# Two layers of windowed attention and MLP on one core: all queues, homes and PSUM banks in a new order, with K's weights and products ahead of Q's

## The chip, the core and the metric

The kernel runs on one core of a Trainium2 chip. Its time is the device time of one execution in microseconds (us); the time of a kernel is the median of several executions.

## The reference

```python
# x: 1 x 2048 x 512 bf16; 32 heads of 16; window W = 256; F = 1792
def A(x, wqkv, wo):                       # sliding-window attention
    q, k, v = split(x @ wqkv)             # each 32 x 2048 x 16
    s = q @ k.T * 16 ** -0.5
    mask = (i - j >= 0) & (i - j < 256)   # query i, key j
    return softmax(where(mask, s, -1e9)) @ v  -> heads joined -> @ wo
def B(x, w1, b1, w2, b2):                 # dense MLP
    return gelu_tanh(x @ w1 + b1) @ w2 + b2
x = A_x
for _ in range(2):                        # the same weights twice
    x = x + A(layernorm(x), wqkv, wo)
    x = x + B(layernorm(x), w1, b1, w2, b2)
```

## The kernel before

The 2048 rows are 16 tiles of 128; two layers make 32 tiles, taken in 16 blocks of two tiles (256 queries). All weights and the activations X stay in SBUF in bf16; sums are made in PSUM, in 8 banks of 512 fp32 columns.

For each block, `lnq` makes the layernorm of X (VectorE's statistics, the reciprocal root on GpSimd, the normalised `xn` on VectorE), transposes it (by DMA; on TensorE for tiles 0 to 3 of the first layer and for the last two of the kernel) into `xnTA`, and multiplies it by Q's weights; `kv` does the same for K and V. One group of Q or of K is 8 products of 256 columns into one bank (L653, operands `Wqkv_sb` and `xnTA`), V is 4 products of 512 columns a tile. Q and V are copied out of PSUM by VectorE or ScalarE (L588, L590); K is copied and masked to even and odd heads by VectorE (L687). `Vs`, V with its halves of 64 rows exchanged, is made by DMA (L702).

`attention(b)` runs score visits: a visit takes four banks in two pairs, makes 512 columns of scores for each of four row groups (L754: products of 64 to 256 columns on 32 rows, four of them side by side), then one exponential on ScalarE for each pair (L761, 128 x 1024), which frees the pair, and a multiplication by 0/1 masks on VectorE or GpSimd (L782). After five visits (three in the first block of a layer) P x V runs for one half of the heads (L804, on rows 64 at a time), VectorE transposes the result out of PSUM (L813), takes reciprocals of the sums (L817), normalises (L821, VectorE or GpSimd) and transposes again; then the output product with `Wo_sb` is added to X (L849) and the second layernorm follows.

`mlp(J)` takes jobs of 2 or 4 tiles (`JOBS`): 14 hidden chunks (L653, `W1_sb` and `xnTB`), of which six go through VectorE's bias addition (L871) and three GELUs of two chunks each, and eight through ScalarE's GELU with bias straight from PSUM (L879). Each output tile is 14 products (L653, `W2_sb` and `gT`, 512 columns) added by VectorE to `Xb` (L894), X plus the second bias; in the second layer it is then written to the output. The last tile is split into two halves of 256 columns. ScalarE's exponentials and GELUs need different tables, so they are grouped: the order has 19 changes of table.

Before the first real product TensorE runs 18 warm-up products of zeros (L539, `warm`, 32 or 512 columns).

No loop sets the order in which all this reaches the engines. The code above only adds nodes to a plan (`_Plan.add`), 3098 of them, and three tables written out by hand set the rest. `_Plan.run` applies them:

```python
for i in _ALT:
    nodes[i]["eng"], nodes[i]["fn"] = nodes[i]["alts"][1]
banks = iter(_BANKS)
for i in _ORDER:
    ...
    for g, k in nd["alloc"]:
        b = next(banks)
        gmap[g] = tuple(range(b, b + k))
```

`_ORDER` is one global order of the nodes; each engine's queue is what that order holds for it. `_ALT` names the nodes that go to their second home: a copy of Q, V or a transposed tile from VectorE to ScalarE, a mask or a normalisation from VectorE to GpSimd, an addition of epsilon from GpSimd to VectorE. `_BANKS` gives each allocation in PSUM its bank, or the first of its pair. `_Sched.op` then adds the semaphore waits that reads, writes and reused banks need, in that order; so an engine waits in its queue where what it needs is late, and all behind it on that engine waits too.

## Time and profile before

| | before |
|---|---|
| median of 3 runs | 442.46 us (442.39 to 442.56) |
| span of the profiled execution | 442.4 us |
| TensorE (PE) busy | 416.1 us, 94% |
| ScalarE (ACT) busy | 386.4 us, 87% |
| VectorE (DVE) busy | 341.0 us, 77% |
| GpSimd (POOL) busy | 212.7 us, 48% |

The profile is of one execution, on this one core. PEld is TensorE's loading of weights, which overlaps its products; SP is the engine whose queue issues the DMAs. In a row of a group, `out<-in` names the tensors, then come partitions x elements and the type, the count, busy time in us and the mean of one in ns, and behind the second bar the idle time just before the group's instructions with what ended most of it. In a row of the timeline stand the start in us, the busy time, the engine, the line, the operation, and in brackets the wait and its releaser. Where a row says `W_sb`, it is W1, W2 or a part of them. The records hold nearly all products of TensorE.

### The profile page before, as it was taken

To read this page: it belongs to the slowest core of one execution; us is meant where nothing else is said; L and a number is where in the kernel's file an instruction comes from. 1 tells how busy PE (TensorE), PEld (TensorE's weight loads), DVE (VectorE), ACT (ScalarE), POOL (GpSimd) and SP (SyncE) were. 2 spreads that over 40 slices of the span, in tenths; PEclk is the share of its full clock that TensorE was granted. 3 is DMA by queue.
4 is the path that set the end of the run, shared out by engine and by line. 5 is a ranking of instruction groups with operands and counts; after the bars stand their busy time and mean duration, and the time that the engine had idled before them with its cause. 6 is when DMAs were issued, how large, how long until landed. Compare 5 with 4: busy or idle time off the path is not lost.

```text
span 442.4 us, 16864 instructions
## 1 busy us (share of the span) xinstructions
PE 416.1 (94%) x7523; PEld 233.2 (53%) x7593; DVE 341.0 (77%) x638; ACT 386.4 (87%) x458; POOL 212.7 (48%) x236
## 2 busy tenths in 40 slices
PE   8997999988789997999999999999999999999997
PEld 4555657544444563554455455455555464444675
DVE  7997789788785599967698868877888576746762
ACT  4997999999889999889899989999897988999533
POOL 3566344363442674711575454634728165804411
PEclk9999999999899999999999999999999999999999
DMA  7686422004101012121031021100421014003002
GB/s 234 184 209 185 87 64 45 20 10 69 39 3 25 16 34 56 28 46 24 4 65 31 1 57 26 34 20 10 69 39 20 20 39 105 14 1 81 15 0 73
DMA packets 48116, 23.25 MB, mean 53 GB/s; under 512 B 33196, under 2 KB 48044, under 8 KB 48044
## 3 DMA queue, kind: packets, MB, share of 16 engines
q1 hardware_dynamic: 48044, 22.17, 22.2%
q8 instruction: 60, 0.98, 0.9%
q14 instruction: 12, 0.10, 0.1%
HBM read 8.00 MB, written 2.10 MB: 23 GB/s over the span
## 4 chain that ended last, share of the span: by engine, by line
PE 79%; ACT 11%; DVE 6%; issue 2%; DMA 1%; DVEq 0%
PE ps L653 59%; PE ps L754 9%; PE ps L804 9%; ACT E L761 9%; DVE OD L813 1%; PE ps L539 1%; DVE stat L599 1%; DVE X L849 1%; DMA xnTB<-xn 1%; ACT gT L879 1%; ACT L879 1%; DVE KT L687 1%; DVE E L782 0%; PE ps L639 0%; ACT QT L590 0%
## 5 line engine op out<-in xcount | busy, mean ns | idle before, releaser
L761 ACT ACTIVATE E<-ps 128x1024 bf16<-128x1024 f32 x300 | 284.2, 1033 | 28.7 <-PE ps L754 28.0
L782 POOL TENSOR_TENSOR E<-E,mask 128x512 bf16<-128x512 bf16 (+2 forms) x111 | 120.9, 1106 | 91.3 <-ACT E L761 91.0
L653 PE MATMUL ps<-W_sb,gT 128*128 128x512 bf16 (+1 forms) x434 | 112.2, 373 | 3.2 <-issue 2.2
L653 PE MATMUL ps<-xnTB,W_sb 128*128 128x512 bf16 (+1 forms) x541 | 107.8, 336 | 3.4 <-issue 1.8
L653 PEld LDWEIGHTS ps<-xnTB,W_sb 128*128 128x128 bf16 x560 | 52.0, 98 | 42.9 <-issue 4.1
L653 PE MATMUL ps<-xnTA,Wqkv_sb 128*128 128x256 bf16 x512 | 70.7, 273 | 0.9 <-ACT E L761 0.4
L782 DVE TENSOR_TENSOR E<-E,mask 128x512 bf16<-128x512 bf16 (+2 forms) x125 | 60.1, 500 | 13.3 <-ACT E L761 12.9
L754 PE MATMUL ps<-QT,KT 32*128 32x128 bf16 (+3 forms) x1920 | 60.3, 231 | 9.8 <-ACT E L761 5.6
L653 PEld LDWEIGHTS ps<-W_sb,gT 128*128 128x128 bf16 x462 | 41.2, 98 | 41.1 <-issue 3.6
L754 PEld LDWEIGHTS ps<-QT,KT 32*128 32x128 bf16 x1920 | 28.5, 92 | 59.1 <-ACT E L761 34.9
L653 PEld LDWEIGHTS ps<-xnTA,Wqkv_sb 128*128 128x128 bf16 x512 | 47.4, 98 | 20.2 <-issue 2.9
L813 DVE STREAM_TRANSPOSE OD<-ps 128x1024 f32<-128x1024 f32 x32 | 39.9, 1246 | 21.3 <-PE ps L804 20.7
L887 POOL TENSOR_TENSOR Xb<-X,b2all 128x512 f32<-128x512 bf16 x32 | 37.7, 1180 | 34.3 <-DVE X L894 33.9
L879 ACT ACTIVATE gT<-ps,b1T 128x512 bf16<-128x512 f32 (+1 forms) x80 | 42.6, 609 | 9.5 <-PE ps L653 9.4
L804 PE MATMUL ps<-E,Va 64*17 64x128 bf16 (+3 forms) x1920 | 44.3, 234 | 1.9 <-issue 0.8
L821 POOL TENSOR_TENSOR Nb<-OD,Rc 128x512 bf16<-128x512 f32 x25 | 26.4, 1058 | 38.7 <-DVE Rc L817 29.8
L804 PE MATMUL ps<-E,Vs 64*17 64x128 bf16 (+3 forms) x1920 | 44.9, 234 | 0.0
L599 DVE BATCH_NORM_STATS2 stat<-X 128x6 f32<-128x512 bf16 x64 | 42.9, 679 | 0.5
L804 PEld LDWEIGHTS ps<-E,Va 64*17 64x17 bf16 x1920 | 37.2, 85 | 11.6 <-issue 9.0
L871 DVE TENSOR_SCALAR gT<-ps,b1T 128x512 bf16<-128x512 f32 (+1 forms) x60 | 36.8, 632 | 6.6 <-PE ps L653 6.2
L687 DVE TENSOR_TENSOR KT<-ps,parmask 128x1024 bf16<-128x1024 f32 x32 | 38.7, 1211 | 3.6 <-PE ps L653 3.6
L804 PEld LDWEIGHTS ps<-E,Vs 64*17 64x17 bf16 x1920 | 38.0, 85 | 0.2
(55 smaller groups left out, 348.8 us busy)
## 6 DMA issues: line engine op xcount, KB each, us to landing
Vs<-Va SPq DMA_DIRECT2D x64, 68.0 KB, 2.0
W_sb<-in_B_w_dram SPq DMA_DIRECT2D x4, 512.0 KB, 4.8
out_dram<-X SPq DMA_DIRECT2D x15, 128.0 KB, 1.8
X<-in_A_x_dram SPq DMA_DIRECT2D x3, 512.0 KB
Wqkv_sb<-in_A_wqkv_dram SPq DMA_DIRECT2D x4, 256.0 KB, 4.5
W_sb<-in_B_w_dram SPq DMA_DIRECT2D x2, 384.0 KB, 7.1
W_sb<-in_B_w_dram SPq DMA_DIRECT2D x1, 768.0 KB, 5.0
Wqkv_sb<-in_A_wqkv_dram SPq DMA_DIRECT2D x1, 512.0 KB, 6.7
```

Of the source, the lines that this page charges most:

```text
L599: add("dve", lambda e, B, t=t, k6=k6: e.bn_stats(stat6[:, k6, :], X[:, t, :]), reads=["X%d" % t], writes=["st%d" % k6], key="bs%d" % (k + j))
L653: r = e.matmul(ps[:, B[g][0], cols], lhsT, rhs, start=st, stop=sp)
L687: add("dve", lambda e, B, g=g, i=i: e.tensor_tensor(out=KT[:, kb, 2 * i : 2 * i + 2].rearrange("p c m a q -> p a (c m) q"), in0=ps[:, B[g] ...
L754: x = e.matmul(ps[:, bk[r], o : o + n], KT[rows, kb, c, m].rearrange("p a q -> p (a q)"), QT[rows, c, q : q + n], start=True, stop=True)
L761: add("act", lambda e, B, g_=g_, gi=gi: e.activation(E[:, 2 * gi : 2 * gi + 2, e0 : e0 + 512], ps[:, B[g_][0] : B[g_][0] + 2, :], AF.Exp, ...
L782: fn = lambda e, B: e.tensor_tensor(out=Ew, in0=Ew, in1=Mw, op=ALU.mult)
L804: x = e.matmul(ps[32 * r : 32 * r + VW, B[g][par], c % 2 * 2 * P + lo : c % 2 * 2 * P + hi], V[rows, (2 * b + m // 2) % VR, c * HC + 2 * r ...
L813: add("dve", lambda e, B: e.transpose(OD[:, s].rearrange("p a c q -> p (a c q)"), ps[:, B[g][0] : B[g][0] + 2, :]), reads=["ps:" + g], wri ...
L821: return e.tensor_tensor(out=Nb[:, s, :].rearrange("p (k a d) -> p a k d", a=2, d=Dh), in0=sums[:, :, :, 0:Dh], in1=rc[:, :, :, None].to_b ...
L871: add("dve", lambda e, B, g=g, fc=fc: e.tensor_scalar(out=gT[:, fc, c0 : c0 + M], in0=ps[:, B[g][0], 0:M], scalar1=b1T[:, fc : fc + 1], sc ...
L879: add("act", lambda e, B, g=g, fc=fc: e.activation(gT[:, fc, c0 : c0 + M], ps[:, B[g][0], 0:M], AF.Gelu_apprx_tanh, bias=b1T[:, fc : fc + ...
L887: add("pool", lambda e, B, t=t, xs=xs: e.tensor_tensor(out=Xb[:, xs, :], in0=X[:, t, :], in1=b2all[:], op=ALU.add), reads=["X%d" % t, "b2a ...
```

## The change

Only the three tables are new; each line of them differs. All else in the file is the same, and as `_ORDER` is seven lines shorter, every later line's number is 7 lower (L653 becomes L646, L754 L747, L761 L754, L804 L797, L782 L775, L539 L532).

```diff
 _ORDER = [
-    15, 34, 5, 0, 6, 14, 35, 7, 33, 28, 38, 29, 47, 8, 18, 23, 9, 36, 3, 26, 31, 10, 57, 37, 11, 22, 1, 40, 4, 24,
+    34, 15, 0, 1, 35, 16, 8, 5, 17, 38, 9, 19, 3, 37, 10, 23, 57, 11, 36, 29, 2, 12, 40, 20, 58, 4, 59, 61, 33, 30,
...
 _ALT = [
-    67, 70, 75, 102, 109, 116, 121, 148, 165, 170, 185, 192, 198, 202, 211, 216, 337, 342, 370, 374, 378, 384, 389,
+    67, 70, 75, 95, 109, 116, 121, 165, 170, 185, 192, 198, 202, 207, 211, 216, 337, 342, 374, 378, 379, 383, 384,
...
 _BANKS = [
-    0, 1, 0, 1, 0, 2, 3, 2, 3, 5, 7, 0, 6, 5, 3, 2, 5, 4, 2, 4, 2, 3, 3, 5, 0, 1, 2, 6, 1, 5, 2, 4, 6, 1, 0, 2, 4, 6,
+    6, 5, 6, 7, 2, 3, 5, 4, 2, 1, 2, 6, 3, 7, 4, 6, 3, 6, 5, 4, 1, 2, 6, 5, 1, 0, 2, 4, 6, 1, 1, 0, 3, 2, 4, 7, 6, 0,
...
```

The homes change in number as follows, over the whole kernel:

| nodes | before | now |
|---|---|---|
| masks: VectorE, GpSimd | 125, 111 | 131, 105 |
| normalisations: VectorE, GpSimd | 7, 25 | 11, 21 |
| copies of Q on ScalarE | 13 | 14 |
| copies of V on ScalarE | 10 | 12 |
| copies of transposed tiles on ScalarE | 3 | 4 |
| additions of epsilon: VectorE, GpSimd | 10, 21 | 13, 18 |

In the queue of DMA issues K's first half of the weights now comes ahead of Q's, and the first bias of the MLP, which stood ahead of both, comes behind all of them. The order of ScalarE's groups of exponentials and GELUs between changes of table is the same.

The order changes in all places. Three of them follow. The first is TensorE's queue at the start: `gT` marks the warm-up products, `xnTA,Wqkv_sb` the products of Q and K of the first block, `ident,xn` a transposition of a tile, `QT,KT` scores. Before:

```order
L539 MATMUL ps<-gT 128x32 x3
L653 MATMUL ps<-xnTA,Wqkv_sb 128x256 x6
L539 MATMUL ps<-gT 128x512
L653 MATMUL ps<-xnTA,Wqkv_sb 128x256 x10
L639 MATMUL ps<-ident,xn 128x128 x4
L653 MATMUL ps<-xnTA,Wqkv_sb 128x256 x2
L639 MATMUL ps<-ident,xn 128x128 x4
L653 MATMUL ps<-xnTA,Wqkv_sb 128x256 x6
L754 MATMUL ps<-QT,KT 128x256 x8
```

Now:

```order
L532 MATMUL ps<-gT 128x512 x2
L646 MATMUL ps<-xnTA,Wqkv_sb 128x256 x16
L632 MATMUL ps<-ident,xn 128x128 x4
L646 MATMUL ps<-xnTA,Wqkv_sb 128x256 x4
L632 MATMUL ps<-ident,xn 128x128 x4
L646 MATMUL ps<-xnTA,Wqkv_sb 128x256 x4
L747 MATMUL ps<-QT,KT 128x256 x8
```

Of the first 16 products, Q's eight came first and K's eight second; now K's come first. The warm-up product that stood behind the sixth of them now stands ahead of the first.

The second place is TensorE's queue in the block whose scores ran at 106 to 116 us; `Wqkv_sb,xnTA` is V, `E,Va` the first rows of P x V. Before:

```order
L754 MATMUL ps<-QT,KT 128x128 x8
L754 MATMUL ps<-QT,KT 128x64 x16
L653 MATMUL ps<-Wqkv_sb,xnTA 128x512 x3
L653 MATMUL ps<-xnTA,Wqkv_sb 128x256 x8
L754 MATMUL ps<-QT,KT 128x256 x16
L653 MATMUL ps<-xnTA,Wqkv_sb 128x256 x8
L754 MATMUL ps<-QT,KT 128x192 x8
L754 MATMUL ps<-QT,KT 128x128 x4
L804 MATMUL ps<-E,Va 17x256 x4
```

Now:

```order
L747 MATMUL ps<-QT,KT 128x64 x16
L646 MATMUL ps<-xnTA,Wqkv_sb 128x256 x4
L747 MATMUL ps<-QT,KT 128x256 x8
L646 MATMUL ps<-xnTA,Wqkv_sb 128x256 x2
L646 MATMUL ps<-Wqkv_sb,xnTA 128x512
L646 MATMUL ps<-xnTA,Wqkv_sb 128x256 x2
L646 MATMUL ps<-Wqkv_sb,xnTA 128x512
L646 MATMUL ps<-xnTA,Wqkv_sb 128x256 x2
L646 MATMUL ps<-Wqkv_sb,xnTA 128x512
L646 MATMUL ps<-xnTA,Wqkv_sb 128x256 x4
L646 MATMUL ps<-Wqkv_sb,xnTA 128x512
L747 MATMUL ps<-QT,KT 128x256 x8
```

Behind the last of these rows now follows `E,Va`, the P x V group. Two visits of eight products each stood back to back, and a third (192 and 128 columns) followed before P x V. Now ten products of 256 and four of 512 columns lie between the two, and the third visit has moved ahead of these rows.

The third place is the end of TensorE's queue; `W2_sb,gT` with 512 columns is an output tile, with 256 columns a half of the last one. Before:

```order
L653 MATMUL ps<-xnTB,W1_sb 128x256 x2
L653 MATMUL ps<-W2_sb,gT 128x256
L653 MATMUL ps<-xnTB,W1_sb 128x256 x2
L653 MATMUL ps<-W2_sb,gT 128x256 x23
L653 MATMUL ps<-W2_sb,gT 128x512 x14
```

Now:

```order
L646 MATMUL ps<-W2_sb,gT 128x512 x4
L646 MATMUL ps<-W2_sb,gT 128x256 x7
L646 MATMUL ps<-W2_sb,gT 128x512
L646 MATMUL ps<-W2_sb,gT 128x256 x3
L646 MATMUL ps<-W2_sb,gT 128x512
L646 MATMUL ps<-W2_sb,gT 128x256
L646 MATMUL ps<-W2_sb,gT 128x512 x2
L646 MATMUL ps<-W2_sb,gT 128x256 x13
```

The last group was a whole tile of 512 columns; now a half of 256 columns is last, and the whole tile's products are spread among the halves'.

## The prediction

> **What bounds the kernel now.** I read the chain that ended last first, then the list of waits, then busy times by stretch.

> ```profile
> PE 79%; ACT 11%; DVE 6%; issue 2%; DMA 1%; DVEq 0%
> ACT E L761 <- PE ps L754: 28.0, 50, 1.8
> PEld ps L754 <- ACT E L761: 34.9, 80, 1.5
> ```

> The chain lies on TensorE for 79% of the span and on ScalarE for 11%. The two rows of waits say why both appear: the exponentials (L761) wait 28.0 us for scores, and the scores (L754) wait 34.9 us for the exponentials, mostly because a score visit needs a PSUM pair that the visit before has just left. So I cut the span where that balance tips. Columns of the next rows are the stretch in us, its length, then busy time of PE, PEld, DVE, ACT and POOL, the granted clock, DMA share and GB/s.

> ```profile
> 10.69:81.70 71.01, 66.52 (x1316) 44.14 (x1326) 61.02 (x117) 66.23 (x87) 35.77 (x40) 1.00 0.51 125
> 81.70:174.50 92.80, 82.61 (x1696) 43.95 (x1710) 73.46 (x139) 86.28 (x96) 49.11 (x51) 0.98 0.15 28
> 174.50:297.80 123.30, 119.22 (x2152) 62.90 (x2173) 98.95 (x183) 113.75 (x130) 59.21 (x62) 1.00 0.16 32
> 297.80:439.30 141.50, 138.49 (x2305) 76.84 (x2329) 98.58 (x179) 114.64 (x139) 64.59 (x68) 1.00 0.16 34
> ```

> Up to 174.5 us ScalarE is busy for 152.5 of 163.8 us and TensorE waits 14.7; from there to 439.3 TensorE is busy for 257.7 of 264.8 us and ScalarE waits 36.4. The front is ScalarE's, the rest TensorE's. A new order can therefore gain where ScalarE idles before 174.5 us (11.3 us in all) and at the two ends; after 174.5 us there are 7.1 us of TensorE's idle time to lose or win, much of it small hand-overs.

> The front's idle time has a simple reading. Each pair of score visits brings TensorE some queued products and ScalarE some exponentials and copies; where TensorE's share is the larger, ScalarE idles by the difference. In the first attention blocks:

> ```profile
> 30.13 0.41 PE L754 MATMUL ps<-QT,KT 32*128 32x128 bf16 x24
> 34.31 1.94 ACT L761 ACTIVATE E<-ps 128x1024 bf16<-128x1024 f32 x2 [0.51 <-PE ps L754]
> 36.91 0.60 ACT L590 ACTIVATE QT<-ps 128x512 bf16<-128x512 f32 x1 [0.67 <-PE ps L653]
> 37.90 0.40 PE L754 MATMUL ps<-QT,KT 32*128 32x256 bf16 x8
> 38.35 1.02 ACT L761 ACTIVATE E<-ps 128x1024 bf16<-128x1024 f32 x1 [0.84 <-PE ps L754]
> ```

> Between the score visits at 30.13 and 37.90 us ScalarE waited 0.51 + 0.67 + 0.84 = 2.0 us. I price TensorE's queue by these:

> ```profile
> 423.74 1.03 PE L653 MATMUL ps<-W_sb,gT 128*128 128x512 bf16 x4
> 428.96 3.00 PE L653 MATMUL ps<-xnTB,W_sb 128*128 128x256 bf16 x26
> 14.33 5.60 ACT L761 ACTIVATE E<-ps 128x1024 bf16<-128x1024 f32 x6
> L653 PE MATMUL ps<-W_sb,gT 128*128 128x512 bf16 x406 | 108.3, 380 | 3.2 <-issue 2.2 <-DVE OD L813 0.2 <-DVE statmv L601 0.2
> ```

> Four products of 512 columns take 1.03 us, of which the last shows its whole 0.38, so one follows another after (1.03 - 0.38) / 3 = 0.22 us; one of 256 columns takes 3.00 / 26 = 0.115; an exponential 5.60 / 6 = 0.93.

> **The change part by part.** Every instruction is kept; TensorE runs the same 7,593 products in both orders, and ScalarE's groups between table loads hold as many exponentials and as many GELUs. What moves is order, homes and banks. The terms:

> *The start.*

> ```profile
> 7.23 0.83 PE L653 MATMUL ps<-xnTA,Wqkv_sb 128*128 128x256 bf16 x6
> 7.90 0.38 PE L539 MATMUL ps<-gT 128*128 128x512 bf16 x1
> 8.29 0.73 DVE L627 TENSOR_SCALAR xn<-X,statmv,rstd 128x512 bf16<-128x512 bf16 x2 [0.76 <-POOL rstd L617]
> 9.40 1.22 DVE L687 TENSOR_TENSOR KT<-ps,parmask 128x1024 bf16<-128x1024 f32 x1 [0.38 <-PE ps L653]
> 10.68 0.12 PEld L754 LDWEIGHTS ps<-QT,KT 32*128 32x128 bf16 x8 [0.28 <-DVE KT L687]
> 11.13 1.94 ACT L761 ACTIVATE E<-ps 128x1024 bf16<-128x1024 f32 x2 [0.91 <-PE ps L754]
> ```

> The first scores wait 0.28 us for K's masked copy, which began at 9.40 when K's products, the second eight, had ended. With K's eight first they end eight products (0.9 us) and a warm-up product (0.2) sooner, so the copy starts when VectorE is through with xn at 9.02 and ends at 10.24. TensorE itself loses the warm-up product (about 0.2) and the wait (0.28). The first exponential comes 0.35 us sooner (0 if the weights land late, 0.45 if nothing else is late).

> *ScalarE's load in the front.* One V copy fewer stands on ScalarE ahead of 174.5 us (17 copies for 18).

> ```profile
> L590 ACT ACTIVATE Va<-ps 128x512 bf16<-128x512 f32 x10 | 6.1, 625 | 1.1 <-PE ps L653 1.0
> L588 DVE CAST Va<-ps 128x512 bf16<-128x512 f32 x22 | 14.8, 676 | 3.4 <-PE ps L653 3.2
> L782 DVE TENSOR_TENSOR E<-E,mask 128x512 bf16<-128x512 bf16 x59 | 29.6, 513 | 4.7 <-ACT E L761 4.6
> L782 POOL TENSOR_TENSOR E<-E,mask 128x512 bf16<-128x512 bf16 x57 | 66.3, 1172 | 52.7 <-ACT E L761 52.7
> L821 DVE TENSOR_TENSOR Nb<-OD,Rc 128x512 bf16<-128x512 f32 x7 | 5.1, 736 | 0.2
> ```

> That is 0.6 us off the engine that sets the front. Its cost on VectorE is 0.68, hidden by VectorE's 29.3 us of idle time in the front. Over the whole kernel ScalarE gets four copies more (30 for 26), so after 174.5 us it has five more, 3.1 us, beside 36.4 us of idle time. I charge 0.4 for them; bounds 0 and 3.1.

> *The half-clock stretch.*

> ```profile
> 112.73 0.40 PE L754 MATMUL ps<-QT,KT 32*128 32x256 bf16 x8
> 114.38 0.40 PE L754 MATMUL ps<-QT,KT 32*128 32x256 bf16 x8 [1.25 <-ACT E L761]
> 116.21 0.40 PE L754 MATMUL ps<-QT,KT 32*128 32x192 bf16 x12 [0.46 <-ACT E L761]
> 121.30 1.94 ACT L761 ACTIVATE E<-ps 128x1024 bf16<-128x1024 f32 x2 [1.78 <-PE ps L754]
> 106.20:109.70 3.50, 2.42 (x31) 1.03 (x32) 2.18 (x5) 3.28 (x5) 2.91 (x3) 1.00 0.50 81
> 113.08:116.49 3.41, 1.70 (x32) 1.02 (x28) 3.07 (x7) 3.41 (x5) 0.25 (x1) 1.00 0.20 41
> 116.49:119.90 3.41, 2.90 (x138) 2.16 (x132) 0.71 (x1) 3.01 (x4) 1.22 (x2) 0.50 0.20 41
> ```

> Two score visits stand back to back, at 112.73 and 114.38, with eight small products before the third. TensorE is busy for only 1.70 of 3.41 us, the next 3.41 us are granted at 0.50, and the P x V group inside them ends late: ScalarE then idles 1.78 us, its longest wait for scores. With 2.42 busy of 3.50 us (106.2) the clock stayed. In the new order 14 products (10 x 0.115 + 4 x 0.22 = 2.0 us, about an exponential pair's length) stand between those two visits, and the P x V group follows the second at once. I take it that no stretch falls to half busy there, and that ScalarE's 1.78 us shrink to 0.3: a gain of 1.5, bounds 0 and 1.8. [...]

> *The other waits of the front.* Between the visits shown at 30.13 and 37.90 the new order has one product of 512 and six of 256 columns fewer: 0.22 + 0.69 = 0.9 us less idle time. Counted the same way, the other nine places where TensorE's share grows hold 7.2 us before and 7.8 now: +0.6 (largest: after the second GELU group, 1.6 for 0.9). Net -0.3, bounds -1.5 and +1.5.

> *The end.*

> ```profile
> 439.39 0.69 DVE L894 TENSOR_TENSOR X<-Xb,ps 128x512 bf16<-128x512 f32 x1 [2.20 <-PE ps L653]
> L894 DVE TENSOR_TENSOR X<-Xb,ps 128x256 bf16<-128x256 f32 x2 | 0.8, 418 | 4.2 <-PE ps L653 4.2
> out_dram<-X SPq DMA_DIRECT2D x15, 128.0 KB, 1.8
> out_dram<-X SPq DMA_DIRECT2D x2, 64.0 KB, 1.7
> ```

> The last group was a whole tile: an addition of 0.69 us, then 128 KB. Now it is half of the split tile: 0.42 us and 64 KB, so 0.27 + 0.1 = 0.35 sooner, bounds 0 and 0.5.

> *Homes of masks and normalisations.* Six masks and four normalisations leave GpSimd (1.17 us for a 512-column mask) for VectorE (0.51). Hidden, as GpSimd and VectorE idle; the price if VectorE's cover is gone is the slower rival.

> Sum on the profiled execution: 442.4 - 0.35 - 0.6 + 0.4 - 1.5 - 0.3 - 0.35 = 439.7 us. That execution's span is 0.06 us under the median of 442.46, so I forecast **439.8 us**.

> **The rivals.**

> *The half-clock stretch stays or moves.* For it: the front still has TensorE waiting 14 us, and both orders set two visits back to back just before 174.5 us. Against it: the clock was full at that place before. The time is 439.8 + 1.5 = 441.3. [...]

> *The order does not do what it says.* K first gains nothing because the weights land late, and the front's waits cancel the rest: 442.4.

> *Slower: VectorE becomes the front's bound.* Ahead of 174.5 us it gets six masks, two normalisations and a Q copy more: 6 x 0.51 + 2 x 0.74 + 0.68 = 5.2 us. It was busy for 134.5 of 163.8 us, so they fit on paper, but K's copies and the P x V transposes release banks from that queue, and a mask in front of one delays scores. If none fits the time is 445.0; it is slower than before from the point where half of it (2.7 us) does not fit. With three quarters it is 443.7.

> **How the numbers follow.** Forecast 0.40; half clock stays 0.17; nothing gained 0.13; VectorE 0.30. About 0.2% (0.9 us) is what a measurement of this kernel can tell from no change. Nearly all of the first case, three quarters of the second and a fifth of the third are faster by more: 0.38 + 0.13 + 0.03 = 0.54. The slower side is the last case and a little: 0.31. Left for within 0.2%: 0.15. The forecast's own range is 438.3 to 441.3 (its bounds added half way). The range of 8 in 10 reaches from 438.3 to 444.0, leaving out the far half of VectorE's case and the luckiest sums. Both signs hold much of the chance.

> **What would show it.** Right: the first exponential at about 10.8 us; no window at clock 0.50 after 10 us; ScalarE idle under 10 us before the two back-to-back visits of the seventh block; after that TensorE busy for 97% as before; the last write half a tile. Wrong: a row of half clock in the front, VectorE over 90% busy in 81.7 to 156 us with P x V or scores waiting for it, or TensorE's idle time after 174.5 us well over 7.1 us, which would mean that the late part, dense before, has lost its cover.

## The result, and the profile after

The changed kernel took **445.15 us** (median of 7, 443.87 to 448.0), the kernel before 442.44 (442.17 to 442.59): a ratio of 1.0078, 95% interval 1.006 to 1.0096. It is slower by 2.7 us where 2.7 us faster was forecast, and outside the range.

Two facts are needed to read any number below. A time holds more than the span of the same execution: 1.7 to 1.9 us in most kernels (445.15 beside 443.4, 448.0 beside 446.3), 1.5 to 1.7 in four of those below (block5_new, block8_new, end_only, start_and_end), up to 2.1 in one (front_old_late_new); so times are compared with times and spans with spans. And in some executions of most kernels a window of 3.41 us is granted half clock; "full clock" below means executions without such a window. Five of the changed kernel's seven are (443.87 to 445.48, median 445.0), two are not (448.0 both; the profiled one is of these).

The chain of the profiled execution after, and its two rows of waits (us in total, times, longest):

```profile
PE 68%; ACT 15%; DVE 8%; DMA 4%; issue 3%; SPq 1%; POOL 0%; DVEq 0%
PEld ps L747 <- ACT E L754: 34.4, 79, 1.1
ACT E L754 <- PE ps L747: 29.5, 50, 3.6
```

TensorE's share fell from 79% to 68%; VectorE, DMA and ScalarE took it. The busy times in two stretches, up to the eighth block's first scores and from there to the end (columns as in the prediction), of the changed kernel:

```profile
0.00:176.16 176.16, 156.86 (x3066) 91.53 (x3091) 150.93 (x288) 158.17 (x190) 79.81 (x95) 1.00 0.32 79
176.16:446.28 270.12, 260.19 (x4456) 140.20 (x4502) 194.90 (x360) 231.70 (x273) 125.53 (x128) 0.99 0.16 35
```

and of the kernel before, from an execution profiled later (the first experiment), in which no window was halved ahead of the end:

```profile
span 440.7 us, 16934 instructions
0.00:173.36 173.36, 160.56 (x3091) 92.63 (x3092) 142.79 (x277) 157.99 (x191) 89.07 (x106) 1.00 0.34 80
173.36:440.70 267.34, 263.27 (x4502) 139.44 (x4502) 198.00 (x362) 228.36 (x268) 123.89 (x130) 1.00 0.16 35
ACT E L761 <- PE ps L754: 9.1, 17, 0.9
```

The same 7,593 weight loads (3091 or 3092 of them in the front) and the same ScalarE work (158.2 for 158.0 us) took 2.8 us longer in the front, and 2.8 longer behind it. VectorE is busy for 8.1 us more ahead of that point (150.9 for 142.8; the prediction counted 5.2), instructions that were held up included. The last row is the wait for scores up to 173.36 us; the changed kernel's, up to 176.16, was 11.2. Behind that point the half-clock window of the changed kernel lies at 178.46 us, in the second stretch; executions with such a window take 3.0 us more (448.0 for 445.0), about as much as this stretch is longer.

Where the front loses it, the timeline shows at three places. The start, in the changed kernel:

```profile
8.01 1.45 POOL L529 MEMSET Va<- 128x320 bf16 x1
8.10 1.90 DVE L620 TENSOR_SCALAR xn<-X,statmv,rstd 128x512 bf16<-128x512 bf16 x2 [0.53 <-POOL rstd L610]
9.92 1.21 DVE L680 TENSOR_TENSOR KT<-ps,parmask 128x1024 bf16<-128x1024 f32 x1
11.18 0.12 PEld L747 LDWEIGHTS ps<-QT,KT 32*128 32x128 bf16 x8 [0.30 <-DVE KT L680]
```

Two normalisations that took 0.73 us before (at 8.29) take 1.90 beside GpSimd's memset of Va, which stood at 1.10 us before. K's masked copy starts at 9.92, not at 9.02 as forecast, and the scores at 11.18, not at 10.33.

The fifth block (scores from 103 us):

```profile
113.26 0.38 PE L646 MATMUL ps<-xnTA,Wqkv_sb 128*128 128x256 bf16 x2 [0.88 <-DVE statmv L594]
117.02 1.22 DVE L680 TENSOR_TENSOR KT<-ps,parmask 128x1024 bf16<-128x1024 f32 x1
117.89 1.15 POOL L775 TENSOR_TENSOR E<-E,mask 128x512 bf16<-128x512 bf16 x1 [2.76 <-ACT E L754]
118.16 1.30 DVE L775 TENSOR_TENSOR E<-E,mask 128x768 bf16<-128x768 bf16 x1
119.61 0.28 PE L797 MATMUL ps<-E,Va 64*17 64x256 bf16 x4 [1.33 <-DVE E L775]
```

and in the kernel before (scores from 101.69 us):

```profile
115.05 1.22 DVE L687 TENSOR_TENSOR KT<-ps,parmask 128x1024 bf16<-128x1024 f32 x1
116.82 0.28 PE L804 MATMUL ps<-E,Va 64*17 64x256 bf16 x4 [0.18 <-ACT QT L590]
```

P x V waits 1.33 us for a mask that stood in VectorE's queue behind K's copy and then took 1.30 us, not 0.55, beside GpSimd's mask; two products of K, ahead of a score visit, wait 0.88 us until VectorE has left their bank (an addition to X that ended at 113.11). The visit of 192 and 128 columns that stood ahead of P x V comes behind it in the new order, not, as the text on the change has it, ahead of the rows shown there. Its scores start at 116.24 us before and at 120.97 now, behind the late P x V, and the exponentials then wait 1.15 us for them.

The eighth block:

```profile
178.00 1.48 PE L646 MATMUL ps<-xnTB,W_sb 128*128 128x512 bf16 x4 [1.41 <-DMA xnTB<-xn]
```

and in the kernel before:

```profile
173.39 0.40 PE L754 MATMUL ps<-QT,KT 32*128 32x256 bf16 x8 [0.73 <-DVE Va L588]
174.17 1.67 PE L653 MATMUL ps<-xnTB,W_sb 128*128 128x512 bf16 x7 [0.38 <-ACT E L761]
```

TensorE waits for transposed tiles behind the block's first scores (176.16): 1.84 us from those scores to the first product, 0.78 in the kernel before.

### The profile page after: what moved, and what is told of

It reads as the page before. It is cut to its first block, busy times and chain, and to the rows that moved or that the text cites. A ratio compares the mean times of both kernels' runs of the same rounds, so it can differ in the third digit from the quotient of the medians.

```text
span 446.3 us, 16863 instructions
## 1 busy us (share of the span) xinstructions
PE 417.1 (93%) x7522; PEld 231.7 (52%) x7593; DVE 345.8 (77%) x647; ACT 389.9 (87%) x462; POOL 205.3 (46%) x223
## 4 chain that ended last, share of the span: by engine, by line
PE 68%; ACT 15%; DVE 8%; DMA 4%; issue 3%; SPq 1%; POOL 0%; DVEq 0%
PE ps L646 53%; ACT E L754 10%; PE ps L747 8%; PE ps L797 8%; DMA xnTB<-xn 3%; ACT gT L872 2%; DVE E L775 2%; DMA xnTA<-xn 1%; DVE OD L806 1%; DVE KT L680 1%; DVE xn L620 1%; DVE stat L592 1%; ACT gT L867 1%; SPq L625 1%; ACT L754 1%
## 5 line engine op out<-in xcount | busy, mean ns | idle before, releaser
L754 ACT ACTIVATE E<-ps 128x1024 bf16<-128x1024 f32 x300 | 284.3, 1034 | 30.1 <-PE ps L747 29.5
L775 POOL TENSOR_TENSOR E<-E,mask 128x512 bf16<-128x512 bf16 (+2 forms) x105 | 116.2, 1119 | 112.6 <-ACT E L754 112.4
L646 PE MATMUL ps<-xnTB,W_sb 128*128 128x512 bf16 (+1 forms) x542 | 109.8, 338 | 4.5 <-DMA xnTB<-xn 2.5
L646 PE MATMUL ps<-W_sb,gT 128*128 128x512 bf16 (+1 forms) x435 | 110.7, 373 | 2.9 <-issue 2.4
L646 PEld LDWEIGHTS ps<-xnTB,W_sb 128*128 128x128 bf16 x560 | 51.8, 98 | 45.1 <-issue 4.6
L646 PE MATMUL ps<-xnTA,Wqkv_sb 128*128 128x256 bf16 x512 | 72.1, 273 | 3.2 <-ACT E L754 1.1
L775 DVE TENSOR_TENSOR E<-E,mask 128x768 bf16<-128x768 bf16 (+2 forms) x131 | 61.1, 490 | 10.4 <-ACT E L754 9.8
L747 PE MATMUL ps<-QT,KT 32*128 32x128 bf16 (+3 forms) x1920 | 60.4, 231 | 7.4 <-ACT E L754 5.2
L646 PEld LDWEIGHTS ps<-W_sb,gT 128*128 128x128 bf16 x462 | 41.4, 98 | 40.9 <-issue 3.0
L646 PEld LDWEIGHTS ps<-xnTA,Wqkv_sb 128*128 128x128 bf16 x512 | 46.5, 98 | 23.0 <-issue 4.4
L747 PEld LDWEIGHTS ps<-QT,KT 32*128 32x128 bf16 x1920 | 28.4, 92 | 57.7 <-ACT E L754 34.4
L806 DVE STREAM_TRANSPOSE OD<-ps 128x1024 f32<-128x1024 f32 x32 | 40.0, 1249 | 19.6 <-PE ps L797 19.5
L872 ACT ACTIVATE gT<-ps,b1T 128x512 bf16<-128x512 f32 (+1 forms) x80 | 43.5, 611 | 7.8 <-PE ps L646 7.7
L864 DVE TENSOR_SCALAR gT<-ps,b1T 128x512 bf16<-128x512 f32 (+1 forms) x60 | 37.3, 635 | 15.6 <-PE ps L646 14.8
L797 PE MATMUL ps<-E,Va 64*17 64x128 bf16 (+3 forms) x1920 | 43.8, 231 | 3.7 <-DVE E L775 2.1
L797 PE MATMUL ps<-E,Vs 64*17 64x128 bf16 (+3 forms) x1920 | 44.5, 231 | 0.0
L797 PEld LDWEIGHTS ps<-E,Va 64*17 64x17 bf16 x1920 | 36.9, 84 | 14.0 <-issue 9.4
L797 PEld LDWEIGHTS ps<-E,Vs 64*17 64x17 bf16 x1920 | 37.7, 84 | 0.3
L814 POOL TENSOR_TENSOR Nb<-OD,Rc 128x512 bf16<-128x512 f32 x21 | 22.6, 1076 | 31.1 <-DVE Rc L810 27.1
## 6 DMA issues: line engine op xcount, KB each, us to landing
out_dram<-X SPq DMA_DIRECT2D x15, 128.0 KB, 2.4
```

Source lines behind the costliest of these rows:

```text
L646: r = e.matmul(ps[:, B[g][0], cols], lhsT, rhs, start=st, stop=sp)
L747: x = e.matmul(ps[:, bk[r], o : o + n], KT[rows, kb, c, m].rearrange("p a q -> p (a q)"), QT[rows, c, q : q + n], start=True, stop=True)
L754: add("act", lambda e, B, g_=g_, gi=gi: e.activation(E[:, 2 * gi : 2 * gi + 2, e0 : e0 + 512], ps[:, B[g_][0] : B[g_][0] + 2, :], AF.Exp, ...
L775: fn = lambda e, B: e.tensor_tensor(out=Ew, in0=Ew, in1=Mw, op=ALU.mult)
L797: x = e.matmul(ps[32 * r : 32 * r + VW, B[g][par], c % 2 * 2 * P + lo : c % 2 * 2 * P + hi], V[rows, (2 * b + m // 2) % VR, c * HC + 2 * r ...
L806: add("dve", lambda e, B: e.transpose(OD[:, s].rearrange("p a c q -> p (a c q)"), ps[:, B[g][0] : B[g][0] + 2, :]), reads=["ps:" + g], wri ...
```

## The experiments

All times are medians in us; "full" is the median of the executions at full clock, "half" how many had a half-clock window. The kernel before, run beside them, had 442.35 to 442.66 (full 442.22 to 442.52). The changed kernel is the row of reference.

| kernel | time | full | half |
|---|---|---|---|
| changed kernel | 445.15 | 445.0 | 2 of 7 |
| before_again | 442.46 | 442.46 | 0 of 11 |
| front_new_late_old | 446.43 | 446.34 | 3 of 5 |
| front_old_late_new | 443.47 | 443.31 | 3 of 12 |
| va_memset_early | 444.92 | 444.80 | 3 of 6 |
| blk4_mask_first | 444.18 | 443.99 | 3 of 12 |
| xn42_early | 446.49 | 446.39 | 3 of 6 |
| front_three_moves | 445.38 | 444.45 | 7 of 12 |
| front_three_moves_late_old | 445.32 | 443.72 | 7 of 12 |
| front_four_moves | 446.73 | none | 6 of 6 |
| start_only | 442.80 | 442.73 | 2 of 12 |
| end_only | 441.95 | 441.94 | 1 of 12 |
| start_and_end | 442.35 | 442.21 | 3 of 12 |
| early_part_new | 442.82 | 442.82 | 0 of 11 |
| block5_new | 444.58 | 443.26 | 5 of 11 |
| block8_new | 443.80 | 442.79 | 6 of 12 |
| tx42_first | 444.04 | 443.92 | 1 of 6 |

**before_again.** No edit.

> The kernel before once more, unchanged, for its span and granted clock beside its time. Theory A (the half-clock stretch is not in most timed executions; the profiled one happened to have it, and a time holds 1.7 us more than the span, as every run of the changed kernel shows: 445.15 beside 443.4, 448.0 beside 446.3): spans of about 440.7 us at a mean granted clock of 1.000 in most executions, times of 442.4; an execution with 0.996 has a span of 442.4 and a time of 444.1. Rival B (the stretch is there in every execution): every span 442.4 at 0.996, and time and span agree to 0.1 us.

Theory A held: span 440.7 beside a time of 442.46, spans of 439.8 to 441.3, no half-clock window in 11 executions. Of all 119 executions of the kernel before, here and beside the other kernels, 19 had at least one. At the place where that profile had its half-clock window, this execution was busier:

```profile
112.50:115.92 3.42, 2.00 (x27) 0.95 (x25) 3.13 (x7) 3.42 (x5) 0.78 (x2) 1.00 0.24 49
115.92:119.33 3.41, 2.91 (x146) 1.99 (x146) 1.58 (x3) 3.40 (x5) 0.62 (x1) 1.00 0.21 43
```

These windows lie 0.6 us earlier against the work than those of the prediction (113.08, 116.49), so 2.00 us of products fell into the first, not 1.70, and the next kept the clock. The same work thus fell differently into the windows of two executions.

**front_new_late_old, front_old_late_new.** The order is cut where both have issued the same set of steps:

```diff
 _ORDER
-steps 1 to 1458 as before
+steps 1 to 1458 as changed
 steps 1459 to 3098 as before
```

> The first 1458 steps of the order (up to the second layer's first exponential, at about 207 us) as changed, with their homes and banks; all later ones as before. Both orders have issued the same set of steps by then. Theory F (the loss is in the front: the start +0.5, VectorE's queue at 112 to 120 us, the late transposes at 176 us; the late part is worth +0.4): 444.5 to 445.0 us without a half-clock stretch, so +2.2 on the kernel before, and up to 448 in executions with one. Rival L (the late part lost its cover): 442.4 to 443.

> The other half: the first 1458 steps as before, all later ones as changed. Theory F: the late part alone costs +0.4, so 442.8 us, and it scatters as little as the kernel before. Rival L: 444.5 to 445 us.

Theory F held for the sign: the front costs 3.8 us at full clock with the old late part, the late part 0.8 with the old front. They do not add to the 2.6 of both together; why the new front is slower with the old late part (two executions at full clock) than with the new one stays open. In its trace all but 0.4 us of the loss lies ahead of 203 us (the table of marks below), so the old late part is not where it is lost.

**va_memset_early.** GpSimd's queue:

```diff
 L524 TENSOR_TENSOR mask<-mask 128x64
+L529 MEMSET Va 128x320
 L610 TENSOR_TENSOR rstd<-rstd,mhalf 128x2
-L529 MEMSET Va 128x320
 L526 TENSOR_SCALAR mask<-mask 128x2x64
```

> The changed kernel with one step of GpSimd's queue moved: the memset that sets the ones in Va (1.45 us) runs right behind the first masks at about 3.0 us, not at 8.0 us beside VectorE's normalisation of x. Theory P (the memset held up VectorE's tensor_scalar, 1.51 us for 0.41, and with it K's masked copy): that row is back at 0.41 us, the first scores start at 10.2 to 10.4 us, not 11.18, and the time falls by 0.8 us to about 444.3. Rival (VectorE was late for another reason, or the front's waits eat the gain): scores still at 11.2, or time unchanged at 445.1.

Theory P held where it is read, at the start (this kernel's line numbers are 15 lower):

```profile
8.12 0.81 DVE L605 TENSOR_SCALAR xn<-X,statmv,rstd 128x512 bf16<-128x512 bf16 x2 [0.53 <-POOL rstd L595]
8.86 1.21 DVE L665 TENSOR_TENSOR KT<-ps,parmask 128x1024 bf16<-128x1024 f32 x1
10.12 0.12 PEld L732 LDWEIGHTS ps<-QT,KT 32*128 32x128 bf16 x8 [0.22 <-DVE KT L665]
```

Two normalisations take 0.81 for 1.90 us and the scores start at 10.12, 1.06 us sooner than in the changed kernel and 0.57 sooner than before. The time fell by 0.2 only (three executions at full clock), and no row shows what took the rest back: in this trace ScalarE's table load behind the second GELU group starts at 80.75 us, at 83.35 in the changed kernel's, but those are single executions.

**blk4_mask_first, xn42_early, front_three_moves, front_three_moves_late_old.** To the memset's move come, in the second of these, the mask of the fifth block ahead of K's copy, and K's first two products behind the visit:

```diff
 L775 TENSOR_TENSOR E<-E,mask 128x4x192
-L680 TENSOR_TENSOR KT<-ps,parmask 128x2x8x64
 L775 TENSOR_TENSOR E<-E,mask 128x4x192
+L680 TENSOR_TENSOR KT<-ps,parmask 128x2x8x64
```

> The changed kernel with the early memset of Va, and two steps moved in the block whose scores run at 103 to 125 us: on VectorE the mask of the fifth visit (it stood behind K's masked copy, 1.22 us, and held up P x V until 119.6) goes ahead of that copy, and on TensorE the first two products of K go behind the fifth visit. Theory Q (VectorE's queue sets this block): from the block's first visit to its ninth 1.3 to 1.5 us less than the 19.5 us with the early memset alone, P x V right behind the seventh visit, and a time 1.4 us lower than with the memset alone, about 443.5. Rival (TensorE's own work and the banks set it; what is gained here comes back as a wait of the exponentials before the next block): under 0.4 us, 444.6 or more.

Half of it: block from first visit to ninth 18.9 us, not 19.5 (18.0 before), and 0.8 us of time at full clock. P x V still waited, now for the other of the two things that VectorE owed it:

```profile
116.13 1.32 POOL L775 TENSOR_TENSOR E<-E,mask 128x512 bf16<-128x512 bf16 x1 [2.29 <-ACT E L754]
116.36 1.22 DVE L680 TENSOR_TENSOR KT<-ps,parmask 128x1024 bf16<-128x1024 f32 x1
117.72 0.28 PE L797 MATMUL ps<-E,Va 64*17 64x256 bf16 x4 [1.21 <-DVE KT L680]
```

K's copy holds a bank that P x V takes, in the old `_BANKS` as in the new; whichever of the two, mask or copy, stands last in VectorE's queue ends that wait.

In xn42_early, VectorE's and GpSimd's queues ahead of the eighth block:

```diff
 L842 TENSOR_TENSOR X<-X,ps 128x512
-L581 CAST Va<-ps 128x32x16
 L592 BN_STATS stat<-X 128x6
 L594 BN_AGGR statmv<-stat 128x2 x2
-L581 CAST Va<-ps 128x32x16
-L592 BN_STATS stat<-X 128x6
+L775 TENSOR_TENSOR E<-E,mask 128x4x192
+L581 CAST Va<-ps 128x32x16 x2
 L620 TENSOR_SCALAR xn<-X,statmv,rstd 128x512 x2
+L592 BN_STATS stat<-X 128x6
```

> The changed kernel with the early memset of Va, and the chain moved that makes the second layernorm's tiles 10 and 11 of the first layer: VectorE's mask back from GpSimd (as in the kernel before), the copy of V and one bn_stats put behind the chain, so that the normalised tiles reach the transposing DMA about 1.2 us sooner. Theory X (TensorE waits at 176 us for these transposes; that wait of 1.8 us costs 1.3 more than before, and it empties TensorE's queue so far that some executions get a half-clock stretch): from the first visit of the eighth block to the fourth 8.8 to 9.2 us (8.5 before, 11.0 with the memset alone in an execution with the stretch, 9.9 without), no execution under 0.997, and a time of 443.6. Rival (the transposes are late for the queue of DMA issues, not for VectorE): the wait stays above 1.5 us and the time at 444.9.

> All three: early memset, mask first in that block, early layernorm chain. If the three causes are separate and are what the changed front lost, times add: 444.9 - 1.4 - 1.3 = 442.2 us, with spans of about 440.5 at a clock of 1.000; level with the kernel before. Rival (one bound behind the other, they cover each other): 443.5 or more.

> The same front with the late part (all behind the first 1458 steps) as before. The old late part alone was 0.6 us of span shorter than the new one behind the old front, so 441.6 us: about 0.9 us under the kernel before, if the late part does not depend on what comes before it. Against that stands that the new front with the old late part was the slowest of all (446.4 for 445.1): by that measure the old late part costs 1.3 here, and the time is 443.5.

Theory X fell. The normalised tiles came 0.3 to 0.6 us sooner and TensorE waited as long, here in the three-move kernel (first scores at 173.97):

```profile
175.68 1.69 PE L646 MATMUL ps<-xnTB,W_sb 128*128 128x512 bf16 x7 [1.31 <-DMA xnTB<-xn]
```

xn42_early was 1.6 us slower at full clock than the memset's move alone (three executions each), which no row explains. The three moves together are 0.35 us faster than the memset's move alone, not 2.7, and with the old late part 443.72, near the second of the two values expected.

**front_four_moves, tx42_first.** The three moves, and in the queue of DMA issues (in the first also VectorE's copies of V behind the normalised tiles):

```diff
-Vs<-Va (tile 15, two halves)
 xnTB<-xn (tile 11)
 xnTB<-xn (tile 10)
+Vs<-Va (tile 15, two halves)
```

> The three moves of before, and in the queue of DMA issues the two transposes of tiles 10 and 11 put ahead of the two DMAs of Vs that stood in front of them; on VectorE the normalised tiles come directly behind the mask. The late part is as changed. In the three-move run these tiles were normalised 0.6 us sooner and TensorE still waited until 1.71 us behind the eighth block's first scores: the transposes had stood behind two Vs issues that waited for a copy of V. Theory S (that queue was the wait): the first MLP product now starts at most 0.9 us behind the first scores (0.78 in the kernel before), the fourth visit 8.4 to 8.7 us behind the first (9.48 in the three-move run), fewer executions at 0.996, and 0.8 us off the 442.7 us that the spans at full clock showed. Rival (transposes slow for another reason): no change.

> The three-move kernel (late part as changed) with one more move: the two transposing DMAs of tiles 10 and 11 go ahead of the two Vs issues in front of them; VectorE's order stays. Theory S (the issue queue sets the wait): they start 0.5 to 1.0 us sooner, TensorE's first product of that job 0.8 to 1.3 us behind the eighth block's first scores (1.71 without), span 442.1 at full clock. Rival (the transposes themselves take what they take and the tiles' buffers come free late): 1.6 to 1.8, span 442.7.

In the first the product came 0.98 us behind the scores, near the 0.9 expected, but a P x V group ahead of them lost 3.6 us:

```profile
170.09 0.73 DVE L620 TENSOR_SCALAR xn<-X,statmv,rstd 128x512 bf16<-128x512 bf16 x2 [2.21 <-DMA xnTB<-xn]
170.74 1.28 DVE L581 CAST Va<-ps 128x512 bf16<-128x512 f32 x2
172.16 0.39 PE L797 MATMUL ps<-E,Va 64*17 64x256 bf16 x4 [3.60 <-DVE Va L581]
```

VectorE stood for 2.21 us at a normalisation whose buffer an earlier transpose had not left, and the copies of V behind it held P x V's bank. So the wait is one of transposes in a row and of four `xn` buffers, not of two Vs issues: in tx42_first, with those alone moved, the product came 1.82 us behind the scores (1.71 without), and the rival held. Its time is 0.5 lower at full clock (five executions each), which the wait named does not explain.

**start_only, end_only, start_and_end.** Pieces of the change in the kernel before:

```diff
 _ORDER
-steps 1 to 161 as before
+steps 1 to 161 as changed, memset of Va early   (start)
 ...
-the last 51 steps as before
+the last 51 steps as changed                    (end)
```

> The kernel before, with the first 161 steps (to about 20 us) in the changed order and homes, K's products first, and with the memset of Va early. Theory (the start's term of the sum was right, but for the memset): first scores at 10.1 to 10.3 us for 10.69, and of that 0.3 to 0.5 us carried to the end: spans of 440.3 for 440.7, 442.1 us. Rival (the transposes of the next tiles, behind weights on the DMA queues, eat it by 45 us): 442.5 and more scatter.

> The kernel before with its last 51 steps in the changed order: the whole tile's products among those of the halves, a half of 256 columns last. Theory (term right): the last addition takes 0.42 us for 0.69, the last write 64 KB, the span 0.35 to 0.45 us less: 442.1 us. Rival (the spread products or the write's latency eat it): 442.5.

> Both, the rest as before: if the two add, 0.7 to 0.9 us under the kernel before, 441.7 us.

The start brought the scores 0.49 us forward and nothing to the end: by the score visits at 22 us the trace was 0.4 behind, and the time is 442.73 at full clock beside 442.22. The end brought 0.28 at full clock (441.94 for 442.22); the ratio of all executions, 0.9986, has an interval of 0.9973 to 1.0, so the time alone is not clear of noise. The traces agree with the term: from the start of the last product with W1 to the end of the last addition 6.26 us pass, 6.53 in the kernel before. Both together are level. end_only has the lowest time of the study, not clear of noise.

**early_part_new, block5_new, block8_new.** One stretch of the new order each, in the kernel before:

```diff
 _ORDER
-steps 1 to 653 as before          (early_part_new)
-steps 653 to 901 as before        (block5_new)
-steps 901 to 1458 as before       (block8_new)
+the same steps as changed
```

At steps 653 and 901 the two orders have not issued quite the same set; the few steps that differ run ahead of the stretch or behind it.

> The kernel before with the first 653 steps (to about 86 us) in the changed order, homes and banks; from there as before. If the stretches add, this holds the start (+0.5) and the transposed tiles that land late under the weights' loading (0 to 1.6 us, another amount in each execution): span 441.4 to 441.9 for 440.7 at full clock, a wide scatter, 443.3 us. Rival (the whole loss of the front comes of later stretches): 442.5.

> The kernel before with steps 653 to 901 (about 86 to 127 us, the fifth block's scores among them) in the changed order, homes and banks; all else as before. Theory (VectorE's queue holds up P x V there): span +1.5 at full clock, 444.0 us, P x V of that block 1.2 us or more later behind the block's first visit than before. Rival (the loss there comes of the late start of the block): 442.5 to 442.8.

> The kernel before with steps 901 to 1458 (about 127 to 207 us) in the changed order, homes and banks; all else as before. Theory (the transposes for the fourth MLP job come late and TensorE waits behind the eighth block's first scores): span +1.0 to +1.4 at full clock, 443.7 us, and more executions with half clock than the kernel before has. Rival (the wait comes of the rows ahead): 442.5 to 442.8.

At full clock, against 442.32 for the kernel before: early part +0.5, fifth block +0.9, eighth block +0.5. With the late part's +0.8 (443.31 for 442.52) that is 2.7, and the changed kernel's loss at full clock is 2.6 (445.0 for 442.4). This agreement does not show that the stretches add: front_new_late_old, which holds the three of the front, lost 3.8, not 1.9. Each was expected somewhat dearer (0.8, 1.5 and 1.2), and the two later stretches brought half-clock windows in 5 of 11 and 6 of 12 executions (3 of 27 in the kernel before beside them), which cost 1.9 and 1.6 us more.

The traces tell the same more finely. ScalarE's table loads come in one order in all kernels, so their starts are marks; in before_again four of them start at 81.50, 140.34, 202.61 and 393.23 us. How much later each comes, in us, one execution each:

| kernel | 81.50 | 140.34 | 202.61 | 393.23 | end of the span |
|---|---|---|---|---|---|
| changed kernel (half clock at 178.46) | 1.85 | 2.78 | 5.16 | 5.45 | 5.53 |
| front_new_late_old | 1.23 | 2.16 | 3.26 | 3.38 | 3.68 |
| early_part_new | 0.36 | 0.20 | 0.34 | 0.34 | 0.34 |
| block5_new | -0.71 | 0.25 | 0.25 | 0.34 | 0.53 |
| block8_new | -0.89 | -1.24 | -0.15 | -0.14 | 0.05 |
| blk4_mask_first | 0.55 | 0.90 | 1.60 | 1.66 | 1.74 |
| front_old_late_new | 0.19 | 0.10 | 0.43 | 0.64 | 0.69 |

Between the first two marks the new fifth block costs 0.93, 0.93 and 0.96 us in its three traces, and 0.35 with the mask first. Between the second and the third the new eighth block costs 1.10, 1.09 and, in blk4_mask_first, 0.70, and 2.38 with the half-clock window; the times gave 0.5 for it, and six executions do not settle which is nearer. Ahead of the first mark the traces lie from -0.89 to 0.19 with the old early part and from 0.36 to 1.85 with the new: the early part differs by more than a microsecond from one trace to another. With the memset early and the rest of the early part new, seven traces lie from -0.87 to 0.55. By the marks most of the early part's loss is thus the memset's; the times of va_memset_early (0.2 us less) do not show it, and this stays open.

In block5_new the mask met GpSimd's the other way round:

```profile
115.06 0.55 DVE L775 TENSOR_TENSOR E<-E,mask 128x768 bf16<-128x768 bf16 x1
115.31 1.32 POOL L775 TENSOR_TENSOR E<-E,mask 128x512 bf16<-128x512 bf16 x1 [2.76 <-ACT E L754]
115.72 0.12 PEld L797 LDWEIGHTS ps<-E,Va 64*17 64x17 bf16 x4 [0.32 <-issue]
```

VectorE's started 0.25 us ahead of GpSimd's and took 0.55; in the changed kernel it started 0.27 behind and took 1.30. P x V waited for neither here. What stayed is the fifth visit, behind K's products and their bank: 10.51 us behind the block's first, as in the changed kernel (9.05 before). In block8_new TensorE's wait for the transposes is there by itself:

```profile
174.22 1.90 PE L646 MATMUL ps<-xnTB,W_sb 128*128 128x512 bf16 x8 [1.64 <-DMA xnTB<-xn]
```

## Why the prediction was wrong

**The sum beside the runs.** Three groups of its terms failed. The half-clock term of 1.5 us was no gain for the median. The front's other terms (start -0.35, ScalarE -0.6, waits -0.3) made -1.25, and its three stretches measured +1.9. The late part's terms (+0.4 and -0.35) made +0.05, and it measured +0.8. That is 1.5 + 3.15 + 0.75 = 5.4 us, and 445.15 - 439.8 is 5.35; the closeness owes something to luck, as the stretches need not add.

**The base.** "That execution's span is 0.06 us under the median" compared two things. An execution with a span of 442.4 has a time of about 444.1; the median's executions have spans of 440.7 and no half-clock window. The profile was of the rare case. So the largest term, the 1.5 us of the half-clock stretch, was a gain against an execution that the median is not made of; without it the sum is 441.3, and the rest of the miss is 3.8 us.

**The half-clock stretch.** The new order did fill that place, as the prediction said. It opened another. Windows of the changed kernel (the gap, then the halved one), of the kernel with the early memset (gap), of the three-move kernel (gap), and of end_only, whose halved window lies in the fifth block:

```profile
175.04:178.46 3.42, 1.37 (x36) 0.66 (x36) 3.12 (x9) 3.42 (x5) 0.26 (x1) 1.00 0.40 75
178.46:181.88 3.42, 3.42 (x55) 1.37 (x61) 1.36 (x3) 1.22 (x2) 2.16 (x2) 0.50 0.55 115
...
172.38:175.79 3.41, 1.50 (x36) 0.74 (x36) 3.14 (x9) 3.41 (x5) 0.32 (x1) 1.00 0.41 74
...
174.48:177.89 3.41, 2.21 (x48) 1.08 (x49) 2.32 (x7) 3.10 (x4) 0.74 (x1) 1.00 0.55 116
...
104.56:107.97 3.41, 1.85 (x42) 0.77 (x30) 1.82 (x4) 2.40 (x4) 1.26 (x2) 1.00 0.43 64
107.97:111.38 3.41, 3.41 (x20) 1.16 (x19) 2.16 (x4) 2.27 (x3) 3.41 (x4) 0.50 0.57 87
```

**The start.** The step that failed is "the copy starts when VectorE is through with xn at 9.02 and ends at 10.24". It moved every step of TensorE and of the DMA queue and forgot GpSimd's: the memset came to stand beside xn. -0.35 became +0.49. With the memset away the step was right (scores 0.57 sooner), but the gain did not reach the end (start_only).

**VectorE as the front's bound.** This rival was named, on the right side, at 443.7 us and 0.30. Its mechanism held at one place, the fifth block: a mask behind K's copy, and banks that VectorE leaves late. Its price was sized by work that does not fit (5.2 us); what cost was not the amount but which step stood last at a hand-over. By itself the block costs 0.9 us at full clock. That the price with none of the work hidden, 445.0, is next to the measured time is luck. No run moved the homes alone, so what comes of the homes and what of the order is not told apart.

**The other waits of the front, and ScalarE's load.** The count of products between visits gave -0.3, and one copy fewer on ScalarE -0.6 (by the traces it is a copy of Q, 9 for 10; V's are 5 in both). The front's waits for scores went from 9.1 to 11.2 us instead. The counting prices TensorE's queue as if all that it needs were there; it has no row for transposed tiles that land late. They were late at two places of the new order: ahead of the eighth block (+0.5 by time, 1.1 by the marks), and in the early part at 32 us, with different waits in two traces of the same early order, the changed kernel's and front_new_late_old's:

```profile
33.51 0.39 PE L646 MATMUL ps<-xnTA,Wqkv_sb 128*128 128x256 bf16 x2 [0.20 <-DMA xnTA<-xn]
```

```profile
34.52 0.39 PE L631 MATMUL ps<-xnTA,Wqkv_sb 128*128 128x256 bf16 x2 [1.25 <-DMA xnTA<-xn]
```

Such a wait may be what scatters the early part: early_part_new took 442.29 to 444.70 at full clock, the kernel before beside it 441.80 to 442.82. No run tests it.

**The end.** Right, as far as the runs can tell: -0.35 with bounds 0 and 0.5, measured -0.28 in time and -0.27 up to the end of the last addition. The changed kernel's last row is the half as forecast:

```profile
443.75 0.42 DVE L887 TENSOR_TENSOR X<-Xb,ps 128x256 bf16<-128x256 f32 x1 [0.23 <-PE ps L646]
```

**The late part.** +0.4 for ScalarE's copies and -0.35 for the end made 0.05; measured +0.8, so some 1.1 us are lost between 207 us and the end. No run here says where. In the trace of front_old_late_new only 0.26 us is lost behind 203 us, and its times at full clock hold 2.0 us more than its spans, 0.25 more than in the kernel before; so a part of the loss may lie outside the span.

## What to carry to other kernels

Before a profile serves as the base of a sum, set its span and its granted clock beside those of several executions: here the one profiled had a loss that the median had not. When an order changes, list for every engine what now runs at the same moment, GpSimd beside VectorE above all, and what each step's buffer and bank must wait for; the work between two visits is a lower bound only. And look for gaps of TensorE of some 1.5 us: in traces here where one fell whole into a window of 3.41 us, half clock could follow, at up to 3.0 us, and whether it falls so differs from one execution to the next. How busy a window must be to keep the clock, these traces do not settle.

## What the runs showed of the hardware

Where GpSimd and VectorE met in these rows, the instruction that started first kept its length and VectorE's, when it came second, took longer: xn of 0.41 us took 1.51 beside a memset of 1.45 (the first of a pair that took 1.90, not 0.73), a mask of 0.55 took 1.30 when it started 0.27 us behind GpSimd's of 1.15, and 0.55 when it started 0.25 ahead (GpSimd's then took 1.32). In the profiles of before and after, 8 of the 128 normalisations took 0.69 to 1.73 us, the others at most 0.46; each of the 8 started 0.04 to 0.62 us behind an operation of GpSimd that was still running. VectorE's masked copies out of PSUM (KT, 1.16 to 1.23 us in the changed kernel) took no longer beside GpSimd's operations than alone (1.19 to 1.23).
